# Windowed attention with a gated feed-forward block on one core: groups of four blocks instead of three, three of four convolutions of the first batch on TensorE, and another written order

## The chip, the core and the metric

The kernel runs on one core of a Trainium2 chip. The metric is the device time of one execution in microseconds (us). Three runs of the kernel before gave a median of 378.64 us (378.25 to 379.29). The engines are called as in the profile: PE is TensorE's matmul, PEld its weight load, DVE is VectorE, ACT is ScalarE, POOL is GpSimd, and SP issues the DMAs. All of them work at the same time, each in its own written order, and wait for one another through semaphores.

## The reference

There are 8 batches, 8 heads, 576 positions and 64 channels per head. The first half is attention over a window of the last 64 positions; the second half is a feed-forward block with a gate made by a causal convolution with 5 taps over positions, one weight per tap and channel:

```python
scores = scale * np.matmul(q, k.transpose(0, 1, 3, 2))
mask = (rel >= 0) & (rel < window)          # rel = query position - key position
scores = np.where(mask, scores, -1000000000.0)
attn = np.exp(scores - max); attn = attn / (sum + 1e-09)
x = attn @ v                                # heads side by side: 8 x 576 x 512
for k in range(K):
    gate_pre += conv_w[k][None, None, :] * xp[:, k:k + S, :]
gate = 1.0 / (1.0 + np.exp(-gate_pre))
out = (gate * (x @ w_val)) @ w_out
```

The three weight arrays arrive as 64-bit floats and are taken apart on the chip.

## The kernel before

**Units and blocks.** Two heads of one batch form a unit, so there are 32 units, four per batch. A unit has 9 blocks of 64 queries; each block needs the keys of its own 64 positions and of the 64 before, so its scores are 64 x 128. A step of attention, numbered m, takes two groups of three blocks (`GB = NB // NG` = 3) for both heads: 6 blocks, 48 steps in all. Two groups lie side by side on the 128 partitions, and the two heads in two tiles. The stages of a step are called S (scores, PE, line 425), M (scale, mask and row maximum, DVE, line 444), X (exponential and row sum, ACT, line 456), Ra and Rb (1 over the sum, POOL and DVE, lines 461 and 466), N (scaling of the exponentials, POOL, line 474), PT (transposes, PE, line 482) and EP (copy out of PSUM to `pts`, ACT or DVE). When all blocks of a unit are there, AV (line 506) multiplies with v.

**Out of attention.** A unit's result `av` in PSUM is rounded into `xh` (XH), the remainder goes to `xl` (XL, line 538), so that the projections can run as three fast products. The convolution (line 564) is one ACT pass for the newest tap and four DVE passes for the others, into `gp`. For the units 0 to 3 `av` is first copied to SBUF (`x`) and the passes read that copy, so that the PSUM tile comes free; for all others they read PSUM. Behind the last unit of a batch the sigmoid (SIG, line 741) runs on ACT, for the batches 0 and 7 in two halves.

**Feed-forward.** Per batch, V (line 602) makes eight tiles 128 x 288 of 12 matmuls each; HF (line 613) multiplies by the gate; HH and HL (lines 198/201 and 631) round the product into `h_hi` and `h_lo`; O (line 663) makes the output tiles of 128 positions, 12 matmuls of 512 columns each; EO copies them out of PSUM and SP stores them. Three PSUM tiles of kind f are shared by V, O and filler matmuls.

**Weights.** Each of eight 512-column parts of the two weight matrices goes through six DVE passes, one ACT pass and two POOL passes (`rest1`, `rest2`, lines 377 and 380) that give a rounded part and a remainder (`wv_hi`, `wv_lo`, `wo_hi`, `wo_lo`). The parts are named w0 to w3 (for V) and w4 to w7 (for O); no O can start before all of w4 to w7.

**The order.** A planner (`in_order`, line 74) walks over all operations with a table of costs, gives each an engine where several are allowed (`flex`), and writes one fixed order per engine; DMAs too. The engines then follow it. In stretches before the first V in which the planner sees PE idle, it puts filler matmuls on PE (`spare`, line 764).

Of the kernel before, what the change touches and what calls it, by code (L numbers as in the profile page):

```python
# [13 lines left out]
ALU = mybir.AluOpType  # L14
# [59 lines left out]
def in_order(ops, room):  # L74
# [25 lines left out]
    while len(out) < total:  # L100
        best = None
        for e, c in ready.items():
            c[:] = [op for op in c if op not in done]
            pick = None
            for op in c:
# [9 lines left out]
                k = (t - (CFG["wait"] if e == "P" and op.prio < CFG["ffn_prio"] else 0), op.rank)  # L115
# [43 lines left out]
def tile_window_attention_gated_ffn(  # L159
# [114 lines left out]
    def load_qk(i):  # L274
# [5 lines left out]
        for n, (j0, j1) in enumerate(zip(cuts, cuts[1:])):  # L280
            def emit(_, n=n, j0=j0, j1=j1):
                if n == 0:
# [6 lines left out]
                            prio=(CFG["lq"] | ({0: CFG["lq0"][n]} if len(cuts) > 2 else {})).get(i, i * NG - 9)))  # L289
        return [loads[sum(g * GB + GB > c for c in cuts[1:-1])] for g in range(NG)]  # L290

    def load_v(i):
# [41 lines left out]
    def split_f64(name, words, rows, n, hi, lo, tag, load, prio, free=()):  # L334
# [41 lines left out]
        def rest1(_):  # L376
            nc.gpsimd.tensor_sub(out=like(t["mf"]), in0=like(t["af"]), in1=hi.bitcast(F32))  # L377

        def rest2(_):
            nc.gpsimd.tensor_add(out=lo, in0=like(t["mf"]), in1=like(t["lf"]))  # L380
# [25 lines left out]
    def where(s):  # L406
        return divmod(s, NG)

    def scores(m):
# [405 lines left out]
```

## Time and profile before

| | us |
|---|---|
| median of 3 runs | 378.64 |
| the profiled execution's own time | 378.58 |
| its span, first to last instruction | 376.8 |
| PE busy in the span | 354.9 |
| DVE busy | 283.7 |
| ACT busy | 264.6 |
| POOL busy | 147.4 |
| filler matmuls (part of PE's busy time) | 25.7 |

The profile is of one execution, 1.8 us shorter in its span than in its own time. Busy PE says nothing of whether the work is useful: the fillers count too, and a matmul at a lower granted clock is busy for longer. The profile cuts the span into 40 slices or into stretches that one asks for, and names for each idle time the instruction that ended it. Because the engines' orders are fixed, a stage is read best by who is never idle in it.

### The profile page before, as it was taken

To read this page: it belongs to the slowest core of one execution; us is meant where nothing else is said; L and a number is where in the kernel's file an instruction comes from. 1 tells how busy PE (TensorE), PEld (TensorE's weight loads), DVE (VectorE), ACT (ScalarE), POOL (GpSimd) and SP (SyncE) were. 2 spreads that over 40 slices of the span, in tenths; PEclk is the share of its full clock that TensorE was granted. 3 is DMA by queue.
4 is the path that set the end of the run, shared out by engine and by line. 5 is a ranking of instruction groups with operands and counts; after the bars stand their busy time and mean duration, and the time that the engine had idled before them with its cause. 6 is when DMAs were issued, how large, how long until landed. Compare 5 with 4: busy or idle time off the path is not lost.

```text
span 376.8 us, 10700 instructions
## 1 busy us (share of the span) xinstructions
PE 354.9 (94%) x3962; PEld 309.1 (82%) x3962; DVE 283.7 (75%) x1002; ACT 264.6 (70%) x837; POOL 147.4 (39%) x226
## 2 busy tenths in 40 slices
PE   8989998773999999999999999999999999999996
PEld 8878887652888997799879988899889987998984
DVE  5869999699987997779659986698668975871510
ACT  2879889776998797678957896778857975341221
POOL 6776864852754344324332344143404430000000
PEclk9999999695899999999999999999999999999999
DMA  8986544240537452634364433735242323002012
GB/s 277 394 294 202 169 125 128 77 151 27 179 108 238 130 177 98 212 128 140 114 207 157 128 127 126 244 101 173 85 158 64 91 95 120 28 2 84 30 57 84
DMA packets 22149, 52.09 MB, mean 138 GB/s; under 512 B 2385, under 2 KB 4945, under 8 KB 22097
## 3 DMA queue, kind: packets, MB, share of 16 engines
q1 hardware_dynamic: 22096, 51.41, 40.8%
q8 instruction: 31, 0.51, 0.6%
q14 instruction: 22, 0.17, 0.1%
HBM read 41.96 MB, written 9.44 MB: 136 GB/s over the span
## 4 chain that ended last, share of the span: by engine, by line
PE 77%; DVE 13%; DMA 4%; issue 1%; POOL 1%; ACT 1%; SPq 1%; DVEq 0%; ACTq 0%; POOLq 0%
PE o L663 27%; PE v L602 25%; PE av L506 10%; PE s L425 8%; PE pt L482 7%; DVE gp L564 5%; DMA ktb<-in_kT_dram 4%; DVE p L444 4%; DVE xl L538 1%; POOL wv_lo L380 1%; POOL w2m L377 0%; DVE pts L201 0%; DVE hf L613 0%; SPq L320 0%; ACT xh L198 0%
## 5 line engine op out<-in xcount | busy, mean ns | idle before, releaser
L456 ACT ACTIVATE p<-p,nm 128x128 f32<-128x128 f32 x288 | 112.3, 394 | 10.5 <-DVE nm L444 6.2
L474 POOL TENSOR_TENSOR p<-p,rc 128x384 f32<-128x384 f32 x96 | 82.2, 874 | 36.6 <-DVE rc L466 34.4
L564 DVE SCALAR_TENSOR_TENSOR gp<-av,cw,gp 128x575 f32<-128x575 f32 (+1 forms) x112 | 90.7, 810 | 4.1 <-ACT gp L562 3.0
L602 PE MATMUL v<-xl,wv_hi 128*128 128x288 f32 x256 | 80.2, 313 | 0.7 <-DVE hf L613 0.7
L602 PE MATMUL v<-xh,wv_hi 128*128 128x288 f32 x256 | 76.1, 297 | 0.0
L602 PE MATMUL v<-xh,wv_lo 128*128 128x288 f32 x256 | 75.9, 296 | 0.0
L444 DVE CUSTOM_DVE_ANT_0 p<-s,mask 128x128 f32<-128x128 f32 x288 | 66.7, 285 | 7.6 <-PE pt L482 5.1
L663 PE MATMUL o<-wo_hi,h_lo 128*128 128x512 f32 x144 | 59.4, 413 | 0.0
L663 PE MATMUL o<-wo_lo,h_hi 128*128 128x512 f32 x144 | 57.0, 396 | 0.0
L663 PE MATMUL o<-wo_hi,h_hi 128*128 128x512 f32 x144 | 57.0, 396 | 0.0
L456 ACT ACTIVATION_READ_ACCUMULATOR p<-p,nm 128x1 f32 x288 | 54.9, 191 | 0.0
L482 PE MATMUL pt<-ident,p 128*128 128x128 f32 x288 | 49.1, 280 | 6.0 <-ACT pts L198 2.8
L602 PEld LDWEIGHTS v<-xl,wv_hi 128*128 128x128 f32 x256 | 48.8, 191 | 3.3 <-issue 2.1
L631 POOL TENSOR_TENSOR h_lo<-hf,h_hi 128x288 fp32r<-128x288 f32 (+2 forms) x41 | 24.6, 610 | 68.1 <-ACT h_hi L198 67.8
L506 PEld LDWEIGHTS av<-pts,v 128*64 128x64 f32 x1152 | 37.9, 143 | 15.4 <-DVE gp L564 9.6
L506 PE MATMUL av<-pts,v 128*64 128x64 f32 x1152 | 42.4, 230 | 8.0 <-DVE gp L564 7.4
L602 PEld LDWEIGHTS v<-xh,wv_hi 128*128 128x128 f32 x256 | 48.8, 191 | 0.0
L602 PEld LDWEIGHTS v<-xh,wv_lo 128*128 128x128 f32 x256 | 48.7, 190 | 0.0
L425 PE MATMUL s<-ktb,qtb 64*64 64x128 f32 x1152 | 46.4, 283 | 2.0 <-DVE nm L444 1.7
L461 POOL TENSOR_SCALAR su<-su 128x6 f32<-128x6 f32 x48 | 13.1, 274 | 88.6 <-ACT p L456 87.3
L482 PEld LDWEIGHTS pt<-ident,p 128*128 128x128 f32 x288 | 34.2, 141 | 13.7 <-POOL p L474 5.9
L198 ACT COPY ot<-o 128x512 f32<-128x512 f32 x32 | 18.6, 582 | 37.0 <-PE o L663 28.1
(120 smaller groups left out, 514.5 us busy)
## 6 DMA issues: line engine op xcount, KB each, us to landing
v<-in_vw_dram SPq DMA_DIRECT2D x32, 576.0 KB, 4.0
out_dram<-ot SPq DMA_DIRECT2D x36, 256.0 KB, 2.1
qtb<-in_qT_dram SPq DMA_DIRECT2D x31, 288.0 KB, 3.9
ktb<-in_kT_dram SPq DMA_DIRECT2D x31, 288.0 KB, 4.3
st<-in_w_val_dram SPq DMA_DIRECT2D x4, 512.0 KB, 4.9
st<-in_w_out_dram SPq DMA_DIRECT2D x2, 1024.0 KB, 12.3
qtb<-in_qT_dram SPq DMA_DIRECT2D x1, 192.0 KB, 4.9
ktb<-in_kT_dram SPq DMA_DIRECT2D x1, 192.0 KB, 4.9
```

The lines of the kernel that those rows point to most:

```text
L198: nc.scalar.copy(out=out, in_=in_)
L425: nc.tensor.matmul(sp_t[m, hh][half * W:half * W + W, t, :], lhsT=held("qt", i)[r, j * W:j * W + W], rhs=held("kt", i)[r, j * W:j * W + P] ...
L444: nc.vector.tensor_tensor_reduce(out=pe[:, t, :], in0=sp_t[u][:, t, :], in1=mk[first], scale=-SCALE, scalar=3.0e38, op0=ALU.add, op1=ALU.m ...
L456: nc.scalar.activation(out=pe[:, t, :], in_=pe[:, t, :], func=AF.Exp, scale=-1.0, bias=nm[:, t:t + 1], accum_out=su[:, t:t + 1])
L461: nc.gpsimd.tensor_scalar_add(out=su_t[m], in0=su_t[m], scalar1=1.0e-9)
L474: nc.gpsimd.tensor_mul(out=pe, in0=pe, in1=rc_t[m][:, hh, :].unsqueeze(2).broadcast_to([P, GB, P]))
L482: nc.tensor.transpose(out=tp[:, t, :], in_=pe[:, t, :], identity=ident)
L506: nc.tensor.matmul(ap[hh * D:(hh + 1) * D, j * W:(j + 1) * W], lhsT=v_t[i][:, hh * NB + j, :], rhs=pts_t[m, hh][:, t, half * W:(half + 1) ...
L564: nc.vector.scalar_tensor_tensor(out=acc, in0=x, scalar=col, in1=acc, op0=ALU.mult, op1=ALU.add)
L602: nc.tensor.matmul(vp_t[u][:, 0:NH], lhsT=w[:, c, js], rhs=x[:, c, hs], start=(a + z == 0), stop=(a + z == NM - 1))
L631: SUB[e](out=h_lo[:, jb, dst:dst + hi - lo], in0=hf_t[u][:, lo:hi], in1=h_hi[:, jb, dst:dst + hi - lo].bitcast(F32))
L663: nc.tensor.matmul(op_t[row], lhsT=h[:, jb, col:col + P], rhs=w[:, jb, :], start=(a + z == 0), stop=(a + z == NM - 1))
```

## The change

**Groups of four blocks.** A group now has four blocks (`gb=4`) and may begin in one unit and end in the next; a step has 8 blocks, and there are 36 steps. Tiles of S, N, PT and EP are 512 columns wide instead of 384. The number of blocks, matmuls, masks and exponentials is as before.

**Convolution on PE.** `conv='KKKP'`: for the units 0, 1 and 2 the five taps become five matmuls per half of the positions, of `x` against a diagonal matrix that holds a tap's 128 weights (`dg`, built by DVE from the identity, one instruction of 640 columns per unit). Two ACT copies bring the result from a PSUM tile of kind f into `gp`. Unit 3 is convolved like the later ones, from PSUM.

**Who does what.** N may go to POOL or ACT (four activations there), EX, CC and XH as listed in `flex`; the weights' two remainder passes to POOL or DVE; HL always to POOL. The sigmoid is whole for every batch.

**The order.** All priorities and load times are other numbers, each kind of operation gets an offset (`off`), and the planner prefers small-tile matmuls (S and AV) when PE is already at small tiles (`stay`). Fillers end before the first operation that takes a tile of kind f, which is now the first convolution matmul instead of the first V.

```diff
--- before.py
+++ after.py
-    sb=dict(p=6, pts=6, v=2, qt=3, kt=3, ot=2, hf=3, w=2, x=4),
+    sb=dict(p=6, pts=6, v=2, qt=3, kt=3, ot=2, hf=3, w=2, x=3),
...
-    sig_prio=-2,
-    flex=dict(EP="AV", EO="AV", HH="AV", XH="AV", HL="GV"),
+    w_prio=[8, 25, 15, -5, 0, 16, 16, 11],
+    sig_prio=2,
+    flex=dict(EP='AV', EO='AV', HH='AV', XH='AV', HL='G', CC='A', N='GA', EX='AV', WR='GV', DG='V'),
+    dg=(-13, 1, -15, -8),
+    gb=4,
...
-    cut=6,
-    gate={0: (0, 2, 4), 7: (0, 2, 4)},
-    lq0=(-100, -98.5),
+    cut=8,
+    gate={},
+    lq0=(-112, -96),
...
+    stay=150,
+    off={'SIG': -0.22, 'XH': 3.84, 'N': 6.49, 'EX': -0.38, 'S': -4.81, 'HH': -3.07, 'HL': 2.41, 'M': -3.04, 'Ra': 1.75, 'PT': -1.55, 'C': -1.89},
-    sbconv=(0, 1, 2, 3),
+    conv='KKKP',
...
-                k = (t - (CFG["wait"] if e == "P" and op.prio < CFG["ffn_prio"] else 0), op.rank)
+                k = (t - (CFG["wait"] if e == "P" and op.prio < CFG["ffn_prio"] else 0)
+                     - (CFG["stay"] if e == "P" and "F" != mode and op.mode != "F" else 0), op.rank)
...
-    NG = 3
-    GB = NB // NG
-    GT = GB * W
+    GB = CFG["gb"]
+    PB = 1.0 / 3
...
+    MUL = {"G": nc.gpsimd.tensor_mul, "V": nc.vector.tensor_mul}
+    ADD = {"G": nc.gpsimd.tensor_add, "V": nc.vector.tensor_add}
...
+        def rest1(e):
+            SUB[e](out=like(t["mf"]), in0=like(t["af"]), in1=hi.bitcast(F32))
+
+        def rest2(e):
+            ADD[e](out=lo, in0=like(t["mf"]), in1=like(t["lf"]))
...
+        r1 = op(name + "r", pick("WR", G=130 + 1065 * c, V=70 + 535 * c), rest1, [hi_, lw], prio=prio, port="VG")
+        r2 = op(name + "s", pick("WR", G=130 + 1065 * c, V=70 + 535 * c), rest2, [r1], free=[(tag, name)], prio=prio,
+                port="VG")
...
-    def where(s):
-        return divmod(s, NG)
+    def where(s, t):
+
+        return divmod(s * GB + t, NB)
...
+        at = [where(s, t) for s in ss for t in range(GB)]
+        last = [i for i, j in at if j == NB - 1]
...
-            def e_n(_, u=u, hh=hh):
-                pe = p_t[u]
-                nc.gpsimd.tensor_mul(out=pe, in0=pe,
-                                     in1=rc_t[m][:, hh, :].unsqueeze(2).broadcast_to([P, GB, P]))
-            no = op(f"N{u}", ("G", 760), e_n, [r2], prio=prio)
+            def e_n(e, u=u, hh=hh):
+                pe, rc = p_t[u], rc_t[m][:, hh, :]
+                if e == "A":
+                    for t in range(GB):
+                        nc.scalar.activation(out=pe[:, t, :], in_=pe[:, t, :], func=AF.Copy, scale=rc[:, t:t + 1])
+                else:
+                    MUL[e](out=pe, in0=pe, in1=rc.unsqueeze(2).broadcast_to([P, GB, P]))
+            no = op(f"N{u}", pick("N", G=130 + 210 * GB, V=70 + 136 * GB, A=220 * GB), e_n, [r2], prio=prio, port="VG")
...
+            for j in range(NB):
+                s, t = divmod(i * NB + j, GB)
+                m, half = divmod(s, 2)
+                for hh in range(2):
+                    nc.tensor.matmul(ap[hh * D:(hh + 1) * D, j * W:(j + 1) * W],
+                                     lhsT=v_t[i][:, hh * NB + j, :],
+                                     rhs=pts_t[m, hh][:, t, half * W:(half + 1) * W], start=True, stop=True)
...
+        way = CFG["conv"][i:i + 1] or "P"
+        apart = way != "P"
...
+        if way in "Kk":
+            last = []
+            end = 0 if way == "K" else 1
+            for half in range(2):
+                def e_cv(_, half=half):
+                    g = gc_t[i, half] = ps("f", [P, 512], f"g{i}_{half}")
+                    for kk in range(TAPS - 1, end - 1, -1):
+                        back = TAPS - 1 - kk
+                        lo = back if half == 0 else 0
+                        nc.tensor.matmul(g[:, lo:NH], lhsT=dg[:, (hp * TAPS + kk) * P:(hp * TAPS + kk + 1) * P],
+                                         rhs=x_t[i][:, half * NH + lo - back:half * NH + NH - back],
+                                         start=back == 0, stop=kk == end)
+                cv = op(f"K{i}_{half}", ("P", 500 * (TAPS - end)), e_cv, [ex, dgo[hp]], take=[("ps_f", (i, half))],
+                        free=[("x", i)] if half and not end else [], prio=cp)
+
...
+                def e_cc(e, half=half):
+                    acc = batch_tile(gp_t, "gp", b, F32)[:, hp, half * NH:(half + 1) * NH]
+                    g = gc_t.pop((i, half))[:, 0:NH]
...
+                        COPY[e](out=acc, in_=g)
...
+    dg = const.tile([P, NCW * P], F32, name="dg")
+    dgo = []
+    for hp in range(NHP):
+        if CFG["conv"][hp:hp + 1] not in ("K", "k"):
+            dgo.append(None)
+            continue
+
+        def e_dg(e, hp=hp):
+            t = slice(hp * TAPS, (hp + 1) * TAPS)
+            MUL[e](out=dg.rearrange("p (t n) -> p t n", n=P)[:, t, :], in0=ident.unsqueeze(1).broadcast_to([P, TAPS, P]),
+                   in1=cw[:, t].unsqueeze(2).broadcast_to([P, TAPS, P]))
+        dgo.append(op(f"DG{hp}", pick("DG", V=740, G=1450), e_dg, [cwo], prio=CFG["dg"][hp], port="VG"))
+
...
-            if o.name.startswith("V"):
+            if any(kind == "ps_f" for kind, _ in o.take):
                 until = 0
```

What it does to the written order, at three places. The first is PE just before the first V of batch 0 (`v0_0_0`). `pt6_0` is the transpose of step 6 for the first head, `g2_1` the convolution of unit 2, second half of the positions; the number behind the last underscore only tells allocations apart, and x3 or x5 counts instructions of one kind. Before:

```order
L482 MATMUL pt6_0_825<-ident_66,p6_0_610 128x128 x3
L764 MATMUL spare_136<-ident_66 128x128 x6
L482 MATMUL pt6_1_853<-ident_66,p6_1_615 128x128 x3
L602 MATMUL v0_0_0_858<-xl0_452,wv_hi_124 128x288
L602 MATMUL v0_0_0_858<-xh0_441,wv_hi_124 128x288
L602 MATMUL v0_0_0_858<-xh0_441,wv_lo_125 128x288
```

After:

```order
L494 MATMUL pt5_0_909<-ident_66,p5_0_674 128x128 x4
L575 MATMUL g2_1_920<-x2_808,dg_134 128x288 x5
L494 MATMUL pt5_1_947<-ident_66,p5_1_691 128x128 x4
L648 MATMUL v0_0_0_954<-xl0_470,wv_hi_124 128x288
L648 MATMUL v0_0_0_954<-xh0_465,wv_hi_124 128x288
L648 MATMUL v0_0_0_954<-xh0_465,wv_lo_125 128x288
```

Where fillers stood, five convolution matmuls stand; the transposes ahead of the first V are now those of step 5.

The second place is PE at the first output tile, `o0`. Before:

```order
L425 MATMUL s18_0_1597<-ktb0_74,qtb0_71 64x128
L425 MATMUL s18_1_1598<-ktb0_74,qtb0_71 64x128
L482 MATMUL pt15_0_1615<-ident_66,p15_0_1372 128x128 x3
L663 MATMUL o0_1622<-wo_hi_126,h_lo_129 128x512
L663 MATMUL o0_1622<-wo_hi_126,h_hi_130 128x512
L663 MATMUL o0_1622<-wo_lo_127,h_hi_130 128x512
```

After:

```order
L648 MATMUL v0_1_3_1246<-xh0_465,wv_hi_124 128x288
L648 MATMUL v0_1_3_1246<-xh0_465,wv_lo_125 128x288
L494 MATMUL pt8_0_1278<-ident_66,p8_0_928 128x128 x4
L709 MATMUL o0_1290<-wo_hi_126,h_lo_129 128x512
L709 MATMUL o0_1290<-wo_hi_126,h_hi_130 128x512
L709 MATMUL o0_1290<-wo_lo_127,h_hi_130 128x512
```

The first output tile came behind the scores of step 18 (six blocks a step, 114 blocks) and the products of unit 8. Now it comes behind the last V of batch 0; by then the scores of steps 0 to 10 (eight blocks a step, 88 blocks) and the products of units 0 to 5 are issued, and 68 transposes instead of 93.

The third place is DVE at the convolution of unit 3 (`gp0`; `gp1` belongs to batch 1, `w5` to `w7` are weight parts). Before:

```order
L564 SCALAR_TENSOR_TENSOR gp0_460<-x3_840,cw_128,gp0_460 128x574
L564 SCALAR_TENSOR_TENSOR gp1_1122<-av6_1308,cw_128,gp1_1122 128x575
L564 SCALAR_TENSOR_TENSOR gp0_460<-x3_840,cw_128,gp0_460 128x573
L564 SCALAR_TENSOR_TENSOR gp1_1122<-av6_1308,cw_128,gp1_1122 128x574
L564 SCALAR_TENSOR_TENSOR gp0_460<-x3_840,cw_128,gp0_460 128x572
L564 SCALAR_TENSOR_TENSOR gp1_1122<-av6_1308,cw_128,gp1_1122 128x573
L350 TENSOR_SCALAR w7m_1362<-w7m_1362 128x512
L564 SCALAR_TENSOR_TENSOR gp1_1122<-av6_1308,cw_128,gp1_1122 128x572
L354 TENSOR_SCALAR w7a_1361<-w7m_1362 128x512
L466 RECIPROCAL rc13_1417<-su13_1255 128x6
```

After:

```order
L610 SCALAR_TENSOR_TENSOR gp0_585<-av3_854,cw_128,gp0_585 128x575
L610 SCALAR_TENSOR_TENSOR gp0_585<-av3_854,cw_128,gp0_585 128x574
L366 SCALAR_TENSOR_TENSOR w5a_845<-st2_224,w5a_845 128x512
L610 SCALAR_TENSOR_TENSOR gp0_585<-av3_854,cw_128,gp0_585 128x573
L370 TENSOR_SCALAR w5m_846<-w5a_845 128x512
L610 SCALAR_TENSOR_TENSOR gp0_585<-av3_854,cw_128,gp0_585 128x572
L374 SCALAR_TENSOR_TENSOR w5l_847<-st2_224,w5m_846 128x512
```

Unit 3's passes read `av3` in PSUM instead of the copy `x3`, they are no longer interleaved with unit 6, and the passes of units 0 to 2 are gone from DVE's order.

More of the change, by code (lines that the diff above doesn't have):

```diff
@@ L249, in op @@
             cost = {cost[0]: cost[1]}
-        o = Op(name, cost, emit, deps, take, free, prio, port, mode)
+        kind = name.rstrip("0123456789_(), ")
+        o = Op(name, cost, emit, deps, take, free, prio + CFG["off"].get(kind, 0), port, mode)
         ops.append(o)
@@ L288, in load_qk @@
                             take=[("qt", i), ("kt", i)] if n == 0 else (),
-                            prio=(CFG["lq"] | ({0: CFG["lq0"][n]} if len(cuts) > 2 else {})).get(i, i * NG - 9)))
-        return [loads[sum(g * GB + GB > c for c in cuts[1:-1])] for g in range(NG)]
+                            prio=(CFG["lq"] | ({0: CFG["lq0"][n]} if len(cuts) > 2 else {})).get(i, i * NB * PB - 9)))
+        return [loads[sum(j >= c for c in cuts[1:-1])] for j in range(NB)]
     def load_v(i):
@@ L441, in e_m @@
                 for t in range(GB):
-                    first = tuple(t == 0 and where(s)[1] == 0 for s in ss)
+                    first = tuple(where(s, t)[1] == 0 for s in ss)
                     nc.vector.tensor_tensor_reduce(
@@ L447, in e_m @@
                         accum_out=nm[:, t:t + 1])
-            mo = op(f"M{u}", ("V", 630), e_m, [so], take=[("p", u)], free=[("ps_s", u)], prio=prio)
+            mo = op(f"M{u}", ("V", 210 * GB), e_m, [so], take=[("p", u)], free=[("ps_s", u)], prio=prio)
             def e_x(_, u=u, hh=hh):
@@ L487, in e_ep @@
                 COPY[e](out=t, in_=pt_t.pop(u))
-            done.append(op(f"EP{u}", pick("EP", A=371, V=465), e_ep, [po], take=[("pts", u)],
+            done.append(op(f"EP{u}", pick("EP", A=51 + 107 * GB, V=60 + 135 * GB), e_ep, [po], take=[("pts", u)],
                           free=[("ps_pt", u)], prio=prio))
@@ L550, in attention @@
             op(f"FR{i}", ("N", 0), e_fr, [ex, xl_o], free=[("ps_av", i)], prio=s)
+            cp = s + CFG["cp0"][i]
             x_ready = [ex]
-            cp = s + CFG["cp0"][CFG["sbconv"].index(i)]
+        else:
+            cp = s
+        if way in "Kk":
[15 more added lines that the diff above has]
+                    g = gc_t.pop((i, half))[:, 0:NH]
+                    if end:
+                        back, lo = TAPS - 1, (1 - half) * (TAPS - 1)
+                        nc.vector.scalar_tensor_tensor(
+                            out=acc[:, lo:], in0=x_t[i][:, half * NH + lo - back:half * NH + NH - back],
+                            scalar=cw[:, hp * TAPS:hp * TAPS + 1], in1=g[:, lo:], op0=ALU.mult, op1=ALU.add)
+                        if lo:
+                            nc.vector.tensor_copy(out=acc[:, 0:lo], in_=g[:, 0:lo])
+                    else:
+                        COPY[e](out=acc, in_=g)
+                    if half:
+                        del x_t[i]
+                last.append(op(f"CC{i}_{half}", pick("CC", A=335, V=369) if not end else ("V", 440 + 70 * (1 - half)),
+                               e_cc, [cv], free=[("ps_f", (i, half))] + ([("x", i)] if half and end else []), prio=cp))
+            return [xh_o, xl_o], last
         def conv(kk):
@@ L574, in attention @@
                    port="VG" if apart else "G")
[L575 removed]
+        return [xh_o, xl_o], [o]
     vp_t, hf_t, ot_t, op_t = {}, {}, {}, {}
@@ L725, in tile_window_attention_gated_ffn @@
         lv_of[i] = lvs[i]
-        for g in range(NG):
-            lq_of[i * NG + g] = lqs[i][g]
+        for j in range(NB):
+            lq_of[i, j] = lqs[i][j]
     for i in range(NT):
-        while prev["m"] * 2 < (i + 1) * NG:
+        while prev["m"] * 2 * GB < (i + 1) * NB:
             scores(prev["m"])
```

70 lines of the change are left out of this document (25 added, 45 removed).

## The prediction

> **What bounds the kernel now.** I read the page's totals and slices first.
>
> ```profile
> span 376.8 us, 10700 instructions
> PE 354.9 (94%) x3962; PEld 309.1 (82%) x3962; DVE 283.7 (75%) x1002; ACT 264.6 (70%) x837; POOL 147.4 (39%) x226
> PE   8989998773999999999999999999999999999996
> DVE  5869999699987997779659986698668975871510
> PEclk9999999695899999999999999999999999999999
> ```
>
> Every slice here is 9.4 us. Two regimes show: from slice 11 (about 104 us) to the end PE is full at a full clock; before, PE has gaps, DVE is the fullest engine and the clock dips in slices 8 to 10. Stretches make this sharper (columns: length, then busy time of PE, PEld, DVE, ACT and POOL, granted clock, DMA share, GB/s).
>
> ```profile
> 0.00:100.24 100.24, 82.69 (x1073) 72.62 (x1077) 86.51 (x330) 76.63 (x265) 64.66 (x92) 0.91 0.54 185
> 28.00:56.00 28.00, 26.71 (x376) 23.56 (x376) 27.72 (x115) 24.11 (x91) 20.62 (x21) 1.00 0.51 165
> 85.00:95.00 10.00, 3.64 (x61) 3.19 (x61) 10.00 (x30) 6.45 (x17) 3.35 (x5) 0.55 0.09 24
> 140.00:180.00 40.00, 40.00 (x470) 34.39 (x469) 31.63 (x122) 31.28 (x105) 14.90 (x23) 1.00 0.46 157
> ```
>
> At 140 to 180 us PE never pauses and DVE and ACT have a fifth to spare. At 28 to 56 us it is DVE that never pauses, and at 85 to 95 us PE stands still while DVE convolves. Where the regimes meet is the first output tile:
>
> ```profile
> 99.55 0.69 DVE L367 SCALAR_TENSOR_TENSOR w7l<-st,w7m 128x512 f32<-128x512 uint32 x1
> ...
> 103.23 1.28 POOL L380 TENSOR_TENSOR wo_lo<-w7m,w7l 128x512 fp32r<-128x512 f32 x1
> ...
> 104.33 0.48 PE L663 MATMUL o<-wo_hi,h_lo 128*128 128x512 f32 x1
> ```
>
> DVE's last pass over the last weight part ends at 100.24, POOL's remainder follows, and the first O starts at 104.33. From there the end is PE work: 376.8 - 104.3 = 272.5 us. The chain of waits gives the prices of that work:
>
> ```profile
> 120.12 1.20 PE av L506 x36
> ...
> 123.71 0.82 PE s L425 x24
> 124.53 1.79 PE v L602 x12
> 126.32 0.33 PE pt L482 x3
> 126.65 1.58 PE v L602 x12
> ...
> 104.57 2.81 PE o L663 x12
> ...
> 359.01 14.06 PE o L663 x60
> ...
> 373.14 0.59 ACT ot L198
> ```
>
> A V tile takes 1.58 us, 1.79 behind small tiles (so 0.21 for the switch), a step's scores of six blocks 0.82, three transposes 0.33, a unit's AV 1.20, an O tile 2.81. So the time is (when the first O can start) + (PE work that is left then), and each edit is worth what it does to one of the two.
>
> **When the first O can start.** The gate stays DVE's weight work: in the new order DVE makes the remainder of w6 itself, last of the four parts for O. I counted DVE's instructions ahead of that point in both orders and priced the difference.
>
> ```profile
> L564 DVE SCALAR_TENSOR_TENSOR gp<-x,cw,gp 128x575 f32<-128x575 f32 (+3 forms) x16 | 15.2, 950 | 0.0
> L564 DVE SCALAR_TENSOR_TENSOR gp<-av,cw,gp 128x575 f32<-128x575 f32 (+3 forms) x15 | 12.1, 808 | 0.8 <-ACT gp L562 0.8
> L538 DVE TENSOR_TENSOR xl<-av,xh 128x576 fp32r<-128x576 f32 x8 | 6.0, 755 | 5.3 <-ACT gp L562 2.9 <-ACT x L198 2.4
> L613 DVE TENSOR_TENSOR hf<-v,gp 128x288 f32<-128x288 f32 x8 | 3.3, 447 | 0.0
> L466 DVE RECIPROCAL rc<-su 128x6 f32<-128x6 f32 x15 | 2.8, 185 | 0.4 <-POOL su L461 0.2
> L201 DVE COPY pts<-pt 128x384 f32<-128x384 f32 x4 | 2.2, 553 | 1.0 <-PE pt L482 1.0
> L359 DVE SCALAR_TENSOR_TENSOR w4a<-st,w4a 128x512 int32<-128x512 int32 x1 | 1.2, 1196 | 0.0
> L359 DVE SCALAR_TENSOR_TENSOR w1a<-st,w1a 128x512 int32<-128x512 int32 x1 | 0.7, 693 | 0.0
> ```
>
> ```profile
> 102.14 0.29 DVE L444 CUSTOM_DVE_ANT_0 p<-s,mask 128x128 f32<-128x128 f32 x1
> 102.35 0.08 DVE L444 DVE_READ_ACCUMULATOR2_ANT nm<- 128x1 f32 x1
> ```
>
> Removed: 16 convolution passes from `x`, 15.2 us; passes from PSUM 14 before, 8 after, 6 x 0.81 = 4.9; mask and maximum of 102 blocks before, 80 after, at a pace of 102.35 - 102.14 = 0.21, 4.7; one HF 0.4 and six reciprocals 1.1. Together 26.3. The removed xl passes (two) and the added xh (two) cancel. Added: three diagonals of 640 columns, which no row shows; between an HF (0.45) and w4a (1.20) each, I take the xl row scaled by columns, 0.84, 2.5 in all. Seven remainder passes of 512 columns now on DVE, between 0.45 and 1.20 each; scaled from the xl row 0.67, together 4.7. Four copies a third wider, 0.7. Together 7.9. So DVE's busy time to the gate is 86.5 - 26.3 + 7.9 = 68.1. Before, DVE idled 100.24 - 86.51 = 13.7 us there; I keep that: 81.8.
>
> A page differs on the seven passes. The spread between w4a and w1a, the same operation on the same shape (1196 and 693 ns), is a wait. The Trainium skill, page "SBUF — State Buffer", section "Who interferes with whom", says that a DVE instruction with two SBUF inputs waits for a GpSimd instruction that reads SBUF, for all of it. The seven passes and the diagonals have two; by that rule at 1.20 each they cost 5 us more than in my sum, and the forecast would be 375. It agrees with `gp<-x` (950) against `gp<-av` (808).
>
> Behind the gate the last V tile's rounding comes in, on ACT and then, always, on POOL:
>
> ```profile
> L198 ACT CAST h_hi<-hf 128x288 fp32r<-128x288 f32 x41 | 17.3, 430 | 17.3 <-DVE hf L613 16.5
> ...
> L456 ACT ACTIVATE p<-p,nm 128x128 f32<-128x128 f32 x288 | 112.3, 394 | 10.5 <-DVE nm L444 6.2 <-POOL p L474 3.8
> ...
> L474 POOL TENSOR_TENSOR p<-p,rc 128x384 f32<-128x384 f32 x96 | 82.2, 874 | 36.6 <-DVE rc L466 34.4 <-PE s L425 2.2
> L631 POOL TENSOR_TENSOR h_lo<-hf,h_hi 128x288 fp32r<-128x288 f32 x19 | 15.2, 806 | 17.4 <-ACT h_hi L198 17.4
> ```
>
> 0.43 + 0.81 = 1.2, so the first O at 83.0.
>
> **Is PE ready by then?** The 30 convolution matmuls are PE's new work. Fillers are of the same 32-bit kind and the trace shows each as two instructions:
>
> ```profile
> 27.25 1.60 PE L764 MATMUL spare<-ident 128*128 128x128 f32 x12
> ...
> 30.74 1.16 PE L764 MATMUL spare<-ident 128*128 128x128 f32 x8
> ```
>
> Four more take 0.44, so 0.11 for 128 columns, 0.25 for 288, 0.50 for a tap, 15 us for 30 taps. (With a fixed part per instruction it would be less; upper end 0.6 a tap, 18.) From the first of them (about 27 us, when unit 0's copy is there) to the first O PE has also 56 score blocks (7.7), 44 transposes (4.8), five AV (6.0), eight V (12.6): 46 us of 56. They fit, in place of fillers, but the cover is thin: 10 us.
>
> The edits without a term: the sigmoid of batch 0 now waits for unit 3's passes, which stand at about 66 us in DVE's count; with V tiles left to make (five at 1.58, and scores and AV between them) that is hidden. N on ACT 27 times as four activations, between 0.19 (the 288 row by columns) and 0.39 each: 21 to 42 us on ACT, covered by its fifth of free time in the stretch row. Loads: one 512 KB weight load goes behind the first q and k; they landed at 7 us, DVE waits for w0 until then anyway, so up to 1 us of gain, not counted. SP's first v load is four DMAs later, and due only at 24 us.
>
> **What is left for PE.** Against before, less attention is done at the first O: 114 - 88 = 26 blocks of scores (26 x 0.82/6 = 3.6), 25 transposes (2.8), three AV (3.6), one V (1.6): +11.6. The preference for staying in small tiles removes almost nothing: runs of small tiles behind that point are 39 before and 37 after, -0.4. So 272.5 + 11.2 = 283.7.
>
> One wait I expect. Attention is three units less ahead, so batch 1's gate is made late. From the gate to the first HF of batch 1 DVE has 40 blocks (8.5), 12 passes (9.7), five xh or xl (3.8), six copies (4.2), five reciprocals and two HF (1.8): 28 us. PE gets by then through four O, three V, three AV, 40 blocks, 36 transposes and some nine switches: 11.2 + 4.7 + 3.6 + 5.5 + 4.0 + 1.9 = 30.9. If DVE idles as it did before (13.7 of 100), 28 become 32.4: PE waits 1.5 us (0 to 6).
>
> **Sum.** 83.0 + 283.7 + 1.5 = 368.2 for the span; the execution's own time is 1.8 above its span (378.6, the same as the median), so 370.
>
> **Rivals.** *PE becomes the opening's bound at a low clock.* Nothing fills PE's gaps behind the first convolution matmul, and a stalled PE loses its clock:
>
> ```profile
> PE av L506 <- DVE gp L564: 7.4, 3, 6.4
> ...
> 91.36 2.19 PE av L506 x36
> ```
>
> After a wait of 6.4 us the same AV takes 2.19 instead of 1.20, and the stretch 85 to 95 has a clock of 0.55. The 46 us of PE work between 27 us and the first O fit until the mean clock falls under 0.71 (then the first O comes at 92, and the gain is gone); at 0.65 they take 71 us, the first O comes at 98, and the time is 98 + 285.2 + 1.8 = 385. For it: each convolution waits for an ACT copy, and scores queue behind it on PE. Against: a full PE keeps its clock (1.00 at 28 to 56 us, 26.7 of 28 busy), and the long wait of before came from DVE's passes that go away. The Trainium skill, "TensorE: Matmul & The Clock Gate", section "Why this matters for your kernels", puts the limit at idle gaps of about 3 us between bursts; the 6.4 us wait agrees, and by it the shorter waits here would cost nothing.
>
> *The lead is too small for good.* If each of the seven later batches waits as batch 1 might at its worst, 1.5 to 2 us, 10 to 14 us go: 378 to 382. Against it stand DVE's 31.6 and ACT's 31.3 of 40; for it that ACT gets the N.
>
> *More gain.* If DVE's idle time shrinks to 6 us, since xl no longer waits behind ACT's newest-tap pass, the first O starts at 75: 362.
>
> **Chances.** The forecast (365 to 375) 0.55, more gain 0.15, the small lead 0.15, PE's clock 0.10, something else near no change 0.05. A comparison can tell about 0.3% from no change here, 1.1 us. Faster 0.80, the same 0.06, slower 0.14. The range 362 to 379 goes from the rival with more gain into the lower half of the small lead.
>
> **What would show it.** Right: the first O at 80 to 86 us, granted clock 0.9 or more in 30 to 80 us, convolution tap at 0.5 us, PE busy all of 110 to 340 us. Wrong: a clock of 0.5 to 0.7 behind 30 us with PE busy (first rival), or PE waiting for HF or xl in every batch (second).

## The result

The changed kernel takes 363.87 us (median of 4 runs, 362.80 to 364.41) against 378.44 us (4 runs) for the kernel before: a ratio of 0.961, with a 95% interval of 0.9579 to 0.9641. The gain is 14.6 us; 8.4 were forecast. The profiled execution took 364.24 us, 1.7 above its span.

The page of the changed kernel, totals and slices of 9.1 us:

```profile
span 362.5 us, 10606 instructions
PE 350.6 (97%) x3962; PEld 306.7 (85%) x3962; DVE 271.0 (75%) x964; ACT 275.8 (76%) x902; POOL 130.8 (36%) x195
...
PE   6999999999999999999999999999999999999995
...
PEclk9999999999999999999999999999999999999999
...
L487 POOL TENSOR_TENSOR p<-p,rc 128x512 f32<-128x512 f32 x45 | 48.3, 1083 | 19.4 <-DVE rc L475 12.7
```

The two regimes of before are one now: PE is full from the second slice on (the page's last row here is POOL's N, 1083 ns each), and the dip of the granted clock is gone. Stretches of the changed kernel (length, then busy time of PE, PEld, DVE, ACT and POOL, granted clock, DMA share, GB/s):

```profile
0.00:75.78 75.78, 69.83 (x888) 60.88 (x889) 66.74 (x267) 64.00 (x232) 38.90 (x59) 1.00 0.62 205
27.00:77.52 50.52, 49.22 (x645) 41.99 (x643) 47.71 (x190) 48.89 (x171) 26.04 (x28) 1.00 0.49 150
110.00:190.00 80.00, 79.52 (x946) 69.49 (x944) 64.77 (x235) 69.20 (x231) 28.32 (x44) 1.00 0.46 150
190.00:340.00 150.00, 149.18 (x1623) 132.24 (x1623) 108.11 (x335) 104.52 (x316) 48.43 (x71) 1.00 0.35 115
```

In the first row DVE idles 75.78 - 66.74 = 9.0 us up to the end of its last weight pass; before it was 13.7. In the second row, from 27 us to the first O, PE idles 1.3 us of 50.5; the first convolution matmul comes at 28.9. The same stretch of the kernel before, to its own first O:

```profile
27.00:104.33 77.33, 62.30 (x857) 53.82 (x850) 71.18 (x261) 64.10 (x215) 50.15 (x57) 0.89 0.41 132
```

There PE idled 15.0 us, at a granted clock of 0.89. The place where the first O starts, in the changed kernel's timeline (start, length, engine):

```profile
75.00 0.78 DVE L387 TENSOR_TENSOR wo_lo<-w6m,w6l 128x512 fp32r<-128x512 f32 x1
...
77.03 0.29 PE L648 MATMUL v<-xh,wv_lo 128*128 128x288 f32 x1
77.17 0.60 PE L494 MATMUL pt<-ident,p 128*128 128x128 f32 x4
77.52 0.47 PE L709 MATMUL o<-wo_hi,h_lo 128*128 128x512 f32 x1
...
75.62 1.61 POOL L677 TENSOR_TENSOR h_lo<-hf,h_hi 128x288 fp32r<-128x288 f32 x2 [0.39 <-ACT h_hi L202]
```

The first O starts at 77.5 instead of 104.3. The weights were ready at 75.8, the rounding of the last tile at 77.2, and PE itself was busy with V and transposes until just then: three things end within 2 us. In the kernel before PE did not wait right ahead of the first O either; its waits, the longest of 6.4 us, lie earlier. From there to the end are 362.5 - 77.5 = 285.0 us, where before it was 272.5, above all because less attention has been done ahead.

### The profile page after: what moved, and what is told of

Read it like the earlier page. It is cut to its first block, busy times and chain, and to the rows that moved or that the text cites. A ratio compares the mean times of both kernels' runs of the same rounds, so it can differ in the third digit from the quotient of the medians.

```text
span 362.5 us, 10606 instructions
## 1 busy us (share of the span) xinstructions
PE 350.6 (97%) x3962; PEld 306.7 (85%) x3962; DVE 271.0 (75%) x964; ACT 275.8 (76%) x902; POOL 130.8 (36%) x195
## 3 DMA queue, kind: packets, MB, share of 16 engines
q1 hardware_dynamic: 22096, 51.41, 42.9%
## 4 chain that ended last, share of the span: by engine, by line
PE 78%; ACT 10%; DVE 7%; DMA 2%; issue 1%; POOL 1%; SPq 0%; ACTq 0%; DVEq 0%
PE o L709 27%; PE v L648 23%; PE av L517 10%; PE pt L494 8%; PE s L434 8%; ACT p L465 4%; PE g L575 3%; ACT p L485 2%; DVE p L453 2%; DMA ktb<-in_kT_dram 2%; DVE gp L610 1%; ACT pts L202 1%; DVE dg L764 1%; ACT gp L800 1%; DVE hf L659 1%
## 5 line engine op out<-in xcount | busy, mean ns | idle before, releaser
L610 DVE SCALAR_TENSOR_TENSOR gp<-av,cw,gp 128x575 f32<-128x575 f32 (+1 forms) x116 | 93.9, 810 | 4.0 <-ACT gp L608 2.8
L677 POOL TENSOR_TENSOR h_lo<-hf,h_hi 128x288 fp32r<-128x288 f32 (+2 forms) x80 | 54.0, 683 | 94.2 <-ACT h_hi L202 73.2
L453 DVE CUSTOM_DVE_ANT_0 p<-s,mask 128x128 f32<-128x128 f32 x288 | 65.5, 285 | 8.7 <-PE s L434 5.0
L487 POOL TENSOR_TENSOR p<-p,rc 128x512 f32<-128x512 f32 x45 | 48.3, 1083 | 19.4 <-DVE rc L475 12.7
L494 PE MATMUL pt<-ident,p 128*128 128x128 f32 x288 | 44.9, 278 | 3.1 <-ACT pts L202 2.1
L470 POOL TENSOR_SCALAR su<-su 128x8 f32<-128x8 f32 x36 | 11.0, 306 | 95.4 <-ACT p L465 94.7
L659 DVE TENSOR_TENSOR hf<-v,gp 128x288 f32<-128x288 f32 x64 | 28.7, 450 | 20.4 <-PE v L648 19.7
L517 PEld LDWEIGHTS av<-pts,v 128*64 128x64 f32 x1152 | 36.2, 138 | 8.4 <-issue 4.2
L434 PE MATMUL s<-ktb,qtb 64*64 64x128 f32 x1152 | 40.3, 276 | 2.5 <-DMA ktb<-in_kT_dram 2.5
L494 PEld LDWEIGHTS pt<-ident,p 128*128 128x128 f32 x288 | 33.4, 140 | 10.9 <-issue 4.0
L517 PE MATMUL av<-pts,v 128*64 128x64 f32 x1152 | 40.6, 225 | 1.2 <-DVE gp L610 0.8
```

The source lines that it names most:

```text
L434: nc.tensor.matmul(sp_t[m, hh][half * W:half * W + W, t, :], lhsT=held("qt", i)[r, j * W:j * W + W], rhs=held("kt", i)[r, j * W:j * W + P] ...
L453: nc.vector.tensor_tensor_reduce(out=pe[:, t, :], in0=sp_t[u][:, t, :], in1=mk[first], scale=-SCALE, scalar=3.0e38, op0=ALU.add, op1=ALU.m ...
L470: nc.gpsimd.tensor_scalar_add(out=su_t[m], in0=su_t[m], scalar1=1.0e-9)
L487: MUL[e](out=pe, in0=pe, in1=rc.unsqueeze(2).broadcast_to([P, GB, P]))
L494: nc.tensor.transpose(out=tp[:, t, :], in_=pe[:, t, :], identity=ident)
L517: nc.tensor.matmul(ap[hh * D:(hh + 1) * D, j * W:(j + 1) * W], lhsT=v_t[i][:, hh * NB + j, :], rhs=pts_t[m, hh][:, t, half * W:(half + 1) ...
```

## The experiments

Each is the changed kernel with a small edit, or the kernel before with a part of the change. PE's idle time below is the length of the stretch from 27 us to the first O, less PE's busy time in it.

### The three parts, alone and in pairs

The change has three parts that can be set apart: the convolution of units 0 to 2 on PE (C), groups of four (G), and everything else, that is the numbers of the order, the loads and who does what (N). Without C, the new numbers convolve units 0 to 2 on DVE from their SBUF copies. Six runs and the two kernels together give all eight combinations. The runs with the numbers of before are made from the changed file. That file with none of the three parts (`gb=3`, `conv='SSSS'`) was not run: on PE it has the written order of the kernel before until far behind the first O, and another one from there on. So a difference of 1 us against the kernel before, like that of C alone, can't be told from it.

C with the numbers of before:

```diff
-    conv='SSSS',
+    conv='KKKS',
```

> The kernel before with one part of the change alone: units 0 to 2 are convolved on PE (unit 3 keeps its SBUF copy and DVE passes), the planner's numbers, groups of three and the engines of each operation as before. Theory (the opening is set by DVE, and taking convolution passes off DVE is the gain): DVE loses 12 passes x 0.95 = 11.4 us and gains three diagonals, 3.1; the first O also comes with 18 blocks and two units less attention ahead, 11.8 us less on DVE; first O at about 84 instead of 104, 8.1 us of PE work deferred: 366 us (363 to 372). Rival (the new numbers of the order are the gain, the convolution only moves): 374 or more.

G with the numbers of before:

```diff
-    gb=3,
+    gb=4,
```

> The kernel before with groups of four blocks alone, all else as before. Theory: the blocks, and so DVE's and PE's work, stay the same; 378 (374 to 381). Rival (fewer, larger steps are the gain): 370 or less.

C and G with the numbers of before:

```diff
-    gb=3,
-    conv='SSSS',
+    gb=4,
+    conv='KKKS',
```

> The kernel before with the convolution of units 0 to 2 on PE and groups of four, the numbers of the order and the engines as before. Theory A (without the new numbers neither part pays): 379 us or more, up to 388. Rival (the two parts need each other, the numbers are secondary): 370 or less.

The changed kernel without C, so N and G:

```diff
-    conv='KKKP',
+    conv='SSSP',
```

> The changed kernel with the convolution of units 0 to 2 back on DVE, from their SBUF copies; the planner orders anew with the same numbers. Theory: DVE gets 12 passes x 0.95 back and loses the diagonals' 3.1, and 8 blocks more lie ahead of the first O (1.7): first O at 87.5, 1.9 us of PE work less behind it: 372 us (368 to 377). Rival (order and groups are the gain): 364 to 367.

The changed kernel without G, so N and C:

```diff
-    gb=4,
+    gb=3,
```

> The changed kernel with groups of three blocks again, all else kept, ordered anew. Theory: 364 to 367, since neither DVE's nor PE's work changes by more than the 12 extra small instructions. Rival (groups of four carry the gain): 371 or more.

The changed kernel without both, so N alone:

```diff
-    gb=4,
-    conv='KKKP',
+    gb=3,
+    conv='SSSP',
```

> The changed kernel with groups of three and with the convolution of units 0 to 2 back on DVE from SBUF copies: what stays is the new numbers of the order and the new choice of engines. Theory A (the parts only pay together: the numbers set an order that needs both): 378 us (375 to 382), no better than before. Theory B (the parts add up in the new order: conv 12 and groups 7 us from the changed kernel's 364): 383 (380 to 386).

Measured, times in us, ratios to the kernel before on the same chip:

| parts | median | ratio (95%) | first O | span - first O | PE idle, 27 us to first O | clock there |
|---|---|---|---|---|---|---|
| none | 378.44 | 1 | 104.3 | 272.5 | 15.0 | 0.89 |
| C | 379.27 | 1.0039 (1.0021 to 1.0057) | 94.9 | 284.2 | 9.5 | 0.92 |
| G | 386.53 | 1.0211 (1.0184 to 1.0238) | 116.0 | 270.9 | 20.1 | 0.81 |
| C, G | 378.09 | 0.9978 (0.9954 to 1.0003) | 96.2 | 280.7 | 8.0 | 0.90 |
| N | 386.25 | 1.0202 (1.0176 to 1.0229) | 105.2 | 281.2 | 18.2 | 0.89 |
| N, G | 375.74 | 0.9932 (0.9911 to 0.9952) | 92.6 | 281.6 | 14.2 | 0.84 |
| N, C | 370.78 | 0.9799 (0.9774 to 0.9824) | 82.4 | 285.0 | 3.8 | 1.00 |
| N, C, G | 363.87 | 0.9610 (0.9579 to 0.9641) | 77.5 | 285.0 | 1.3 | 1.00 |

All but the median and the ratio are read from one profiled execution each; those of C, G and N took 380.85, 388.69 and 388.18 us, somewhat more than the median. The rows behind the last two columns, in the order C; G; C and G; N; N and G; N and C:

```profile
27.00:94.90 67.90, 58.45 (x693) 47.88 (x694) 55.49 (x204) 54.04 (x181) 42.64 (x50) 0.92 0.39 127
```

```profile
27.00:116.00 89.00, 68.86 (x882) 59.67 (x882) 74.95 (x285) 70.10 (x231) 51.55 (x54) 0.81 0.37 122
```

```profile
27.00:96.20 69.20, 61.24 (x760) 51.19 (x761) 63.22 (x221) 57.09 (x195) 44.85 (x46) 0.90 0.42 133
```

```profile
27.00:105.20 78.20, 60.02 (x818) 49.92 (x813) 71.66 (x249) 62.64 (x223) 30.58 (x40) 0.89 0.41 126
```

```profile
27.00:92.60 65.60, 51.42 (x688) 45.15 (x680) 60.78 (x225) 53.84 (x196) 29.31 (x31) 0.84 0.38 121
```

```profile
27.00:82.40 55.40, 51.56 (x666) 42.64 (x665) 52.92 (x204) 52.01 (x184) 26.64 (x34) 1.00 0.43 138
```

Three things follow. **No part gains alone.** C is level or a little slower, and G and N each cost 2%. Together they give 3.9%. **The worth of a part depends on the others.** By differences of the ratios, times 378.4 us (plus is slower), C is worth +1.5 us with the old numbers and groups of three, -8.8 with the old numbers and groups of four, -15.3 and -12.2 with the new numbers; G is +8.0 on the kernel before and -7.2 beside N and C; N is +7.6 alone and -13.9 beside C and G. **The account holds all the same.** The time is the first O plus what follows it. That is PE's work nearly alone (PE idles 4 to 8 us in it in every run here), and it moves only between 271 and 286 us. It is larger the less attention was done ahead, so a first O that comes 9.4 us earlier (C alone) can bring no gain at all: C alone has 11.7 us more behind it, 8.1 of them for 18 blocks of scores, 15 transposes, two AV and one V tile not yet done (by the prediction's prices).

What sorts the rows is the last two columns. Of the four kernels with the convolution on PE, in order of time, PE idles 1.3, 3.8, 8.0 and 9.5 us; of the four without it 14.2, 15.0, 18.2 and 20.1. The convolution on PE adds 15 us of PE work, and pays when it stops more idle time, fillers and slow matmuls than that. PE's whole span shows it, each instruction counted from its start to the next one's (so that overlapping ends are not counted twice). "Same matmuls" are all that both kernels of a pair have; times in us, here plus is time saved:

| C added to | idle | fillers | same matmuls | convolution | span of the profiled execution |
|---|---|---|---|---|---|
| the kernel before | +4.6 | +8.9 | -0.8 | -15.0 | -2.3 |
| G | +11.4 | +6.0 | +7.7 | -15.1 | +10.0 |
| N | +15.2 | +9.4 | +9.5 | -15.1 | +19.0 |
| N, G | +10.4 | +9.2 | +7.2 | -15.1 | +11.7 |

How the idle time is paid for without C shows in the waits of PE for N and G (total, times, longest), and in PE's timeline behind the wait:

```profile
PE v L648 <- DVE hf L659: 9.8, 1, 9.8
```

```profile
79.76 0.61 PE L648 MATMUL v<-xl,wv_hi 128*128 128x288 f32 x1 [9.79 <-DVE hf L659]
...
83.28 0.44 PE L648 MATMUL v<-xh,wv_lo 128*128 128x288 f32 x1
83.52 0.38 PE L648 MATMUL v<-xl,wv_hi 128*128 128x288 f32 x1
83.74 0.29 PE L648 MATMUL v<-xh,wv_hi 128*128 128x288 f32 x1
83.87 0.30 PE L648 MATMUL v<-xh,wv_lo 128*128 128x288 f32 x1
```

PE stands 9.8 us until DVE has convolved; then the matmuls start every 0.24 us for 3.8 us, and every 0.13 after that. So the long wait is followed by matmuls at half pace, as the kernel before had it behind its 6.4 us wait.

### Is PE or DVE the bound of the new opening?

The prediction gave PE's work a cover of 10 us. Doing each of the 30 convolution matmuls twice adds 15 us to PE and nothing elsewhere. The second pass starts the sum anew, so that the result is computed twice.

```diff
-                    for kk in range(TAPS - 1, end - 1, -1):
+                    for kk in 2 * list(range(TAPS - 1, end - 1, -1)):
```

> The changed kernel in its own order, with each convolution half computed twice on PE (the second pass overwrites the first; 15 us of PE work more between 29 and 56 us). If the prediction's cover of 10 us on PE is there: 369. If PE, which is busy 49.2 of 50.5 us there, bounds the opening by itself: 378 or more.

One run took 376.45 us, at a span of 374.7, with the first O at 89.6: 12.1 us later than in the changed kernel, and 12.2 us more span. That is near the 378 of no cover: of 15 us only 3 were hidden, to about 1 us, since it is one run. Its stretch from 27 us to the first O:

```profile
27.00:89.58 62.58, 62.22 (x679) 52.17 (x672) 46.37 (x188) 48.89 (x169) 24.73 (x28) 1.00 0.38 120
```

PE idles 0.4 us of 62.6, and DVE, which idled 2.8 of 50.5 in the changed kernel, now 16.2. In the changed kernel both engines are nearly full there, and so is ACT (48.9 of 50.5). More work for PE is at once paid for: PE's cover is 3 us. What more work for DVE or ACT alone would cost was not tried. The price of the matmuls in the changed kernel's chain of waits:

```profile
29.07 2.48 PE g L575 x10
31.55 1.20 PE av L517 x36
32.75 1.03 PE s L434 x32
```

Ten instructions are five taps: 0.50 us for a tap.

### What N consists of

Four runs of the changed kernel with one thing of N put back or moved. The order is made anew with each, so all that follows moves too.

The weight parts' old priorities:

```diff
-    w_prio=[8, 25, 15, -5, 0, 16, 16, 11],
+    w_prio=[20, 10, 6, 3, 11, 12, 14, 20],
```

> The changed kernel with the eight weight parts' priorities of before, all other numbers new. Theory (the weight parts' place in DVE's order is what lets V and O start early): first O 8 to 15 us later, less what PE did ahead by then (4 us): 368 to 376. Rival (offsets and loads do it): 364 to 367.

364.85 us, a ratio of 0.9659 (0.9623 to 0.9694) to before: 1 us slower than the changed kernel, and the intervals overlap. The theory that the weights' order carries a large part of N falls. The first O comes at 82.3, 4.8 us later, but the rest is 280.7 and not 285.0, since by then 16 more blocks of scores, 8 more transposes and one more AV are done (2.2 + 0.9 + 1.2 = 4.3 us by the prices in the prediction). PE idles 2.3 us in its stretch. The first O alone isn't the measure; PE's idle time comes nearer to it.

No offsets of the kinds of operation:

```diff
-    off={'SIG': -0.22, 'XH': 3.84, 'N': 6.49, 'EX': -0.38, 'S': -4.81, 'HH': -3.07, 'HL': 2.41, 'M': -3.04, 'Ra': 1.75, 'PT': -1.55, 'C': -1.89},
+    off={},
```

> The changed kernel without the offsets per kind of operation, all other numbers new. Theory (the weight parts' priorities do it, the offsets are fine tuning): 364 to 367. Rival (the offsets decide): 370 or more.

369.11 us, 0.9772 (0.9740 to 0.9804): the offsets are worth 5 us, which lies between what the two theories gave. PE idles 4.0 us to a first O at 83.8.

All N on POOL:

```diff
-    flex=dict(..., N='GA', ...),
+    flex=dict(..., N='G', ...),
```

> The changed kernel with all scaling of the exponentials (N) on POOL, none on ACT; ordered anew with the same numbers. ACT loses 108 activations (ACT was busy 48.9 of 50.5 us between 27 us and the first O, POOL 26). Theory (in the opening PE, DVE and ACT are all full, and the order is fitted to this division): the first O comes later with more attention ahead of it; 364 to 372. Rival (ACT is what holds the opening): 361 or less.

374.69 us, 0.9910 (0.9885 to 0.9935), 10.8 us slower than the changed kernel, where the rival had it faster and the theory too expected less. The first O comes at 91.4, and PE idles 8.0 us before it. Its longest wait from 30 us on:

```profile
PE pt L494 <- POOL p L487: 4.4, 2, 4.0
```

It is that of the transposes for POOL's N. A pass of 512 columns takes POOL 1.08 us in the changed kernel, a quarter more than the 0.87 of 384 columns before. So N on ACT, which the prediction had left without a term, seems to be one of the parts that keep PE busy. How much of the 10.8 us is N's and how much comes from ordering anew was not told apart; the next run shows that ordering anew alone can cost a lot.

The diagonals on POOL instead of DVE:

```diff
-    flex=dict(..., DG='V'),
+    flex=dict(..., DG='G'),
```

> The changed kernel with the three diagonals built by POOL instead of DVE (3.1 us on DVE at 20 to 23 us, in the chain of waits there); ordered anew. Theory (the chain through DVE sets when the convolutions can begin, and PE is full from there on): up to 3 us less, 361 to 364. Rival (the fitted order is lost by any new planning): 366 to 375.

372.16 us, 0.9845 (0.9817 to 0.9873), within the rival's 366 to 375. DVE loses three instructions (3.1 us), and the time grows by 8.3. The planner, with the same numbers, makes another order: the first O at 90.3, PE idle for 7.1 us, its longest waits those for transposes' copies. Numbers fitted to one set of prices were no longer good for another here.

### The fillers

```diff
-    awake=(3000, 120000, 300, 250),
+    awake=(3000, 0, 300, 250),
```

> The changed kernel without any filler matmul. Theory (fillers only keep PE's clock up until the convolutions fill it): the clock falls in the first 27 us, the scores and transposes there take twice as long, PE is warm again by 35 us: plus 1 to 3 us, 365 to 367. Rival (DVE and the loads set the first 27 us, the clock does not matter): 364. Second rival (the order stays late, and a low clock goes on): 370 or more.

Without filler matmuls it takes 365.47 us, 0.9664 (0.9639 to 0.9689): 1.6 us slower than with them, an interval that overlaps by a hair. The first O comes at 79.7. The opening without fillers, as a stretch:

```profile
8.00:30.00 22.00, 13.92 (x148) 10.70 (x148) 19.26 (x80) 16.65 (x68) 8.23 (x10) 1.00 0.84 306
```

The two largest groups of PE's instructions in it (busy, mean ns, idle before):

```profile
L434 PE MATMUL s<-ktb,qtb 64*64 64x128 f32 x92 | 7.0, 423 | 4.7 <-DVE cwm L357 4.5 <-DVE cwm L370 0.2
L494 PE MATMUL pt<-ident,p 128*128 128x128 f32 x20 | 5.8, 441 | 3.4 <-ACT p L485 2.5 <-DVE pts L205 0.9
```

The same groups with fillers, in the changed kernel:

```profile
L434 PE MATMUL s<-ktb,qtb 64*64 64x128 f32 x128 | 4.7, 275 | 2.5 <-DMA ktb<-in_kT_dram 2.5
L494 PE MATMUL pt<-ident,p 128*128 128x128 f32 x24 | 4.1, 285 | 0.7 <-DVE pts L205 0.7
```

Without them a matmul of the scores takes 423 ns instead of 275, so fillers do keep PE fast; but before 27 us PE has so little to do that this costs 1.6 us of the total only.

## Why the prediction was right and where it was wrong

The measured 363.87 us lies below the 365 to 375 of the forecast, which had a chance of 0.55, and within the wider range of 362 to 379.

**The account was right.** That the end is the first O plus PE's work behind it has held in every kernel here, with that work between 271 and 286 us. It was put at 283.7 + 1.5 = 285.2, and it was 285.0. The work done ahead was counted rightly (26 blocks, 25 transposes, three AV and one V less). The 1.5 us of waiting was right in size by luck: PE idles some 2 us more there than before, but never for the gate of batch 1. Its waits behind the first O are these:

```profile
PE pt L494 <- ACT pts L202: 0.8, 1, 0.8
PE av L517 <- DVE gp L610: 0.8, 1, 0.8
PE av L517 <- PE o L709: 0.4, 1, 0.4
```

The prices of its terms held: a step of eight blocks 1.03, 1.20 for an AV, 1.58 to 1.60 for a V tile, 2.81 for an O tile.

**The step that failed: "I keep that", DVE's 13.7 us of idle time.** The first O was put at 83.0 and came at 77.5; this is the whole miss of 5.7 us in the span. The gate came at 75.8, not 81.8. DVE's busy time to it was 66.7 where 68.1 was counted, which gives 1.4; the idle time was 9.0, which gives 4.7; and from the gate to the first O it took 1.7 instead of 1.2, which takes 0.5 back. DVE's three longest waits to the gate in the changed kernel:

```profile
DVE w0m L352 <- DMA st<-in_w_val_dram: 3.2, 1, 3.2
DVE p L453 <- PE s L434: 2.5, 4, 1.7
DVE xl L550 <- ACT x L202: 1.4, 1, 1.4
```

The row of before in the prediction had `xl` waiting 5.3 us for ACT's newest-tap pass and copy (2.9 and 2.4). Now it is 1.4, and the pass is no longer among the waits. That is the mechanism of the rival "more gain", which had 0.15 and put the idle time at 6 and the time at 362; the truth lies nearer to it than to the forecast. Idle time with named releasers is no constant: those that the change removes should have been taken off it, row by row. The 2.9 and 1.0 of the 2.4 are 3.9 of the 4.7, and stood there to be read.

**"They fit, but the cover is thin: 10 us" was wrong in its size.** The work counted, 46 us, was 49.2 busy: 64 blocks of scores were left at 27 us and not 56, 48 transposes and not 44, and eight V tiles took 13.6 us with the switches from small tiles, which the prediction had priced itself at 0.21 and left out here. The stretch was 50.5 us and not 56. PE has 3 us of cover in the changed opening: twice the convolution cost 12 of its 15 us. That DVE's bound and PE's met at nearly the same place was luck, and so the sum was not spoiled; had DVE idled less still, PE's work would have held the first O at 76 or later, not at the 75 of the rival.

**"The groups of four" had no price, and "staying ... removes almost nothing".** The prediction costed the groups through wider copies alone, and gave the new order a price only through DVE's count. Measured beside N and C, the groups are worth 7.2 us, and on the kernel before they cost 8.0. A part of the 7.2 stands in PE's small matmuls: counted from start to start, a scores matmul takes 33.0 ns on average instead of 34.9 with groups of three, a transpose 108 instead of 112, 3.4 us over the whole kernel. PE idles 2.3 us less besides. Beside the groups and C, all of N is worth 13.9; taking back one thing of the new numbers costs 5 us (the offsets) or 10.8 (the scaling, stage N, split between POOL and ACT), each time with another order. What staying in small tiles gives by itself wasn't tried. The removal of DVE passes, which the prediction made the cause, carries most of the gain and is not enough for it: without it 2.7 of the 14.6 us are left, and with the old numbers it moved the first O from 104.3 to 94.9 and gained nothing, because PE still idled 9.5 us at a clock of 0.92 and had 11.7 us more to do behind.

**Where the 14.3 us of span came from.** Counted as in the table of pairs, PE idled 21.9 us before and 11.9 now: 10.0. The fillers went from 24.6 to 15.5: 9.1. The convolution takes 15.1 back. The other matmuls, the same in number and shape, took 330.3 and take 320.1: 10.2. 10.0 + 9.1 - 15.1 + 10.2 = 14.2, with rounding. About half of the 10.2 is the lost clock of before, as two stretches show in which the granted clock was 0.50, and one ahead of the first:

```profile
62.00:69.00 7.00, 4.54 (x46) 3.18 (x45) 6.16 (x26) 5.69 (x22) 5.23 (x6) 1.00 0.01 4
69.00:75.82 6.82, 5.98 (x67) 5.54 (x68) 3.89 (x15) 4.23 (x13) 5.66 (x9) 0.50 0.43 128
86.06:96.30 10.24, 4.94 (x66) 4.49 (x67) 9.49 (x24) 6.68 (x15) 4.42 (x5) 0.50 0.16 52
```

PE was busy for 5.98 + 4.94 = 10.9 us in the two; at the full clock that work would take about half, so some 5.5 us were lost (an estimate). Most of the rest is what the groups of four save in small matmuls, 3.4; a little over 1 us stays open.

**The rivals.** PE at a low clock (0.10) fell: the granted clock is 1.00 in every stretch from 27 us to 340, and the V tiles take 1.58 to 1.60 us. But one argument against it does not hold, that "the shorter waits here would cost nothing". In the kernel before the clock fell to 0.50 at 69.0, and in the 7 us ahead of that PE was busy 4.54 us and waited several times, at the longest here:

```profile
67.95 0.55 PE L482 MATMUL pt<-ident,p 128*128 128x128 f32 x3 [1.47 <-POOL p L474]
```

So waits of at most 1.5 us, close together, were followed by the half clock too. The small lead (0.15) fell: PE idles 0.5 of 80 us at 110 to 190 and 0.8 of 150 behind. N on ACT was bounded at 21 to 42 us; its 108 activations last 394 ns each on average, but overlap, and keep ACT busy for 34.1 us in all:

```profile
L485 ACT ACTIVATE p<-p,rc 128x128 f32<-128x128 f32 x108 | 34.1, 394 | 2.1 <-DVE rc L475 2.0
```

ACT had that time, as the prediction said, but its idle time fell to 11 us of 80 in the stretch 110 to 190.

**The seven remainder passes were right for a reason that the prediction did not give.** Taken at 0.67, they were 676 to 692 ns, one of them 782; the 1.20 by the rule that the prediction cites, and with it 375 us, did not come. But that rule is not refuted. The diagonals by their line (min, median and max ns, first and last start), then POOL's passes over N at 20.5 and 42.9 us, and DVE's instructions that began just ahead of them:

```profile
L764 DVE TENSOR_TENSOR dg<-ident,cw x3: 772/812/1661, 20.3 to 22.6; 128x640 f32<-128x640 f32 x3
```

```profile
20.48 1.50 POOL L487 TENSOR_TENSOR p<-p,rc 128x512 f32<-128x512 f32 x1 [0.32 <-DVE rc L475]
```

```profile
20.32 0.77 DVE L764 TENSOR_TENSOR dg<-ident,cw 128x640 f32<-128x640 f32 x1
```

```profile
42.91 1.43 POOL L487 TENSOR_TENSOR p<-p,rc 128x512 f32<-128x512 f32 x1 [3.12 <-PE g L575]
```

```profile
42.75 0.69 DVE L384 TENSOR_TENSOR w4m<-w4a,wo_hi 128x512 f32<-128x512 f32 x1
```

Three of the four remainder passes of the other line:

```profile
L387 DVE TENSOR_TENSOR wv_lo<-w0m,w0l x1: 689/689/689, 11.1 to 11.1; 128x512 fp32r<-128x512 f32 x1
...
L387 DVE TENSOR_TENSOR wv_lo<-w2m,w2l x1: 676/676/676, 23.9 to 23.9; 128x512 fp32r<-128x512 f32 x1
...
L387 DVE TENSOR_TENSOR wo_lo<-w6m,w6l x1: 782/782/782, 75.0 to 75.0; 128x512 fp32r<-128x512 f32 x1
```

The first diagonal began 0.16 us ahead of the POOL pass and took its 0.77; that POOL pass took 1.50 against a mean of 1.08 on the page. The second began at 21.0, inside the POOL pass, and took 1.66. The remainder pass at 42.75 also began ahead of a POOL pass: it took 0.69, and POOL's pass 1.43. So whichever began first was not slowed, and the other one was. The Trainium skill, page "SBUF — State Buffer", section "Who interferes with whom", has this as a lock on the shared port pair, held for a whole instruction, for a DVE instruction with two SBUF inputs and a GpSimd one that reads SBUF, and says that the order of issue decides who waits; these rows agree with it. The prediction had DVE alone wait. Of the seven passes three met nothing on POOL, the others a pass of 8 columns, one that they held up, or, at 75.0, the end of one (782 ns). One diagonal did wait, so the three were 3.1 us instead of the 2.5 of the sum.

## What to carry to other kernels

When work moves from one engine to another in a fixed order, price the receiver's idle time, its fillers and its lost clock in that stretch against the work it gets, and expect the order to have to be set anew: here each part alone was level or slower, and all together 3.9% faster. Do not carry an engine's idle time over as a constant; split it by what ended each wait, and strike out the waits whose cause the change removes. And where two engines are forecast to be ready within a few us of each other, double the work of the second: it shows which of them is the bound, and how much cover there is.

## What was not expected of the hardware

The granted clock in the stretch rows can read 1.00 while matmuls run slowly. Without fillers the row for 8 to 30 us says 1.00, and in it a scores matmul takes 423 ns against 275 with fillers. The reason is in the trace: its first record of the clock, a full one, is at 30.65 us in that run, and at 6.45 us in the changed kernel. Ahead of the first record a row shows 1.00 without one. Behind the 9.8 us wait of the kernel with N and G, in contrast, there are records, and the row shows the loss:

```profile
70.00:90.00 20.00, 10.24 (x90) 10.01 (x91) 16.76 (x35) 12.47 (x32) 11.74 (x12) 0.66 0.16 46
```

The clock row's dips were real here wherever they were compared with an instruction's duration, but a full reading at the start of a program said nothing; the duration of a known instruction is the better witness. The Trainium skill, page "TensorE: Matmul & The Clock Gate", section "Seeing it yourself", warns that the trace's events of the clock gate have been seen to be unreliable. In these two runs the events fit the durations; what misleads is the time ahead of the first one.
